# Transposing each head's row maxima one head slot later, and splitting the scaling of v over two slots, in a fused attention and MoE kernel

## The chip, the cores and the metric

The kernel runs on one core of one Trainium2 chip. The metric is the time of one execution in microseconds (us) on the device; the median of a few runs is compared.

The engines are named as in the profile: PE is TensorE's matrix multiplication and PEld its weight loads, DVE is VectorE, ACT is ScalarE, POOL is GpSimd, SP is SyncE, which here only issues transfers. Each engine works through its own list of instructions in order, and waits where an instruction needs a result that another engine or a transfer has not delivered.

## The reference

```python
def _attn_ref(q, k, v):                     # 8 batches, 8 heads, 576 positions, 64 columns
    scores = scale * np.matmul(q, k.transpose(0, 1, 3, 2))
    mask = block_i >= block_j               # blocks of 64 positions
    scores = np.where(mask, scores, -1000000000.0)
    scores = scores - np.max(scores, axis=-1, keepdims=True)
    attn = np.exp(scores)
    attn = attn / (np.sum(attn, axis=-1, keepdims=True) + 1e-09)
    return np.matmul(attn, v).astype(np.float32)

def _moe_ref(x, w_in, w_out):               # 4608 tokens, 512 columns, 2048 inner columns
    h = x @ w_in
    sp = np.maximum(h, 0.0) + np.log1p(np.exp(-np.abs(h)))
    g = h * erf(sp)
    return (g @ w_out).astype(np.float32)
```

The second function gets the first one's result with the heads side by side. Inputs and results are f32; the weights come in as f64.

## The kernel before

Matrix products are made from a high and a low part of each operand, so that three products stand for one. The program has one list of 64 heads (8 batches of 8). For head `n`, `load_qk(n)` brings q and k into one of four buffers `qk0` to `qk3` (`n % 4`), `maxes(n)` makes scores in PSUM (PE, tiles `s01`, `s2`, `s3`, `s4`) and reduces each row to its maximum (DVE, L327, tile `mx`, two of them, used in turn). The last step of `maxes` is `e()`: DVE combines two columns of `mx` (L352), PE transposes `mx` (L354, tile `mt`), ACT copies the result out of PSUM (L356), and ACT issues a transfer of 2.5 KB (L357) that writes it as one more row into the q part of the head's buffer. `probs(n)` then makes the scores again, transposed (PE, L370 and L371, tiles `t0` to `t4`): L370 reads that row, so that the maximum is already subtracted, and ACT takes the exponential (L375). ACT and DVE split the result into a high and a low part (`ph`, L381, and `pl`, L382). `pv` multiplies by v (PE, L414, tile `u`) and sums the rows (PE, L437, tile `us`) for two heads at a time; `normalise` divides, and stores x for the MoE.

v is used in groups of four heads, a quad. `load_v` brings v for a quad into the one buffer `v32`. `prep_v` finds the largest magnitude: a reduction on DVE (L276, tile `vm`), a transpose on PE (L278, `vt`), three small DVE instructions (L280 to L282, `vs`), then a PE product that broadcasts the value to all partitions (L284, `vb`), a copy by DVE (L286, `vsb`), and the scaled high and low parts `vh` (ACT, L291) and `vl` (DVE, L292). `vl` is the last reader of `v32`, so the next quad's load waits for it.

The main loop goes over head slots `n`. Slot `n` holds the load of head `n + 3`, `maxes(n + 2)`, `probs(n)`, parts of `pv` and `normalise` of earlier heads, the preparation of the first six weight blocks (`w1`, slots 1 to 8), and a step of `moe1`. In `merge`, each list of steps is spread over a stretch of the slot (from `lo` to `hi`, 0 to 1 unless said). A scheduler then decides each engine's order of instructions: it takes an instruction early where it believes its inputs ready, so MoE matmuls (L154, tile `m_h`, and L164, tile `o`) of later steps stand between those of attention. After the heads comes the rest of the first MoE pass, with six of the sixteen weight blocks, and then the second pass with the other ten. While no x is there, `warm` matmuls (L510) that compute nothing fill PE.

Of the kernel before, what the change touches and what calls it, by code (L numbers as in the profile page):

```python
# [34 lines left out]
def tile_attention_moe(ctx: ExitStack, tc: tile.TileContext, qk, v, w, maskrows, sels, out):  # L35
# [10 lines left out]
    NQ = H // 4  # L46
# [131 lines left out]
    def merge(*lists):  # L178
        for step in merged(*lists):
            step()  # L180
# [11 lines left out]
    N = B * H  # L192
# [46 lines left out]
    with tc.tile_pool(name="apool", bufs=2) as apool, tc.tile_pool(name="spool", bufs=1) as spool, \  # L239
# [17 lines left out]
        def bank(name):  # L257

            turn.append(0)
            k = len(turn) % 8 if not xs1 else 0  # L260
            if k in (2, 5):
                return ps_h.tile([P, 512], F32, tag="h", name=name)
            if k in (3,):
                return ps_o.tile([P, 512], F32, tag="o", name=name)
            return ps_a.tile([P, 512], F32, tag="a", name=name)

        def load_v(b, qd):
            v32 = apool.tile([P, 4, 5 * D], F32, tag="v32", name=f"v32_{b}_{qd}", bufs=1)
            nc.sync.dma_start(v32, v[b, :, 4 * qd : 4 * qd + 4, :])
            return v32  # L270

        def prep_v(b, qd, v32):

            nm = f"{b}_{qd}"
            vm = apool.tile([P, 1], F32, tag="vm", name=f"vm{nm}")
            nc.vector.tensor_reduce(out=vm, in_=v32, axis=AX.XY, op=ALU.max, apply_absolute_value=True)  # L276
            pt = bank(f"vt{nm}")
            nc.tensor.transpose(out=pt[:1, :P], in_=vm, identity=ident)  # L278
            vs = apool.tile([1, 2], F32, tag="vs", name=f"vs{nm}")
            nc.vector.tensor_reduce(out=vs[:, :1], in_=pt[:1, :P], axis=AX.X, op=ALU.max)  # L280
            nc.vector.tensor_scalar(out=vs[:, :1], in0=vs[:, :1], scalar1=1e-30, op0=ALU.max, scalar2=None)
            nc.vector.reciprocal(out=vs[:, 1:2], in_=vs[:, :1])  # L282
            pb = bank(f"vb{nm}")
            nc.tensor.matmul(pb[:, :2], lhsT=onesrow, rhs=vs, start=True, stop=True)  # L284
            vsb = apool.tile([P, 2], F32, tag="vsb", name=f"vsb{nm}", bufs=3)
            nc.vector.tensor_copy(vsb, pb[:, :2])  # L286
            vh = apool.tile([P, 4, 5, D], F16, tag="vh", name=f"vh{nm}")
            vl = apool.tile([P, 4, 5, D], F16, tag="vl", name=f"vl{nm}")
            vf = v32.rearrange("p a b -> p (a b)")
            vhf = vh.rearrange("p a b c -> p (a b c)")  # L290
            nc.scalar.activation(vhf, vf, AF.Copy, scale=vsb[:, 1:2])  # L291
            nc.vector.scalar_tensor_tensor(out=vl.rearrange("p a b c -> p (a b c)"), in0=vf, scalar=vsb[:, 1:2], in1=vhf,  # L292
                                           op0=ALU.mult, op1=ALU.subtract)
            return vsb, vh, vl
# [5 lines left out]
        def load_qk(n):  # L300
            b, h = divmod(n, H)
            t = qks[n % NB][:, : 4 * S].rearrange("p (i n) -> p i n", n=S)
            st = apool.tile([P, S], F32, tag="st", name=f"st_{n}", bufs=3)

            def a():
                nc.sync.dma_start(st, qk[b, h])
                nc.gpsimd.dma_start(t[:D, 2:4, :], qk[b, h].rearrange("(s d) n -> d s n", d=D))
                nc.sync.dma_start(f32(t[D:, 0:2, :]), f32(t[:D, 2:4, :]))
                nc.sync.dma_start(f32(t[:D, 1, :]), f32(t[:D, 3, :]))

            def c():
                nc.gpsimd.tensor_tensor(out=t[:D, 0, :], in0=st[:D, :], in1=f32(t[:D, 2, :]), op=ALU.subtract)  # L312
                nc.gpsimd.tensor_tensor(out=t[D:, 1, :], in0=st[D:, :], in1=f32(t[D:, 1, :]), op=ALU.subtract)  # L313

            return a, c
# [160 lines left out]
        vs, prs, usbs = {}, {}, {}  # L476
        normals, ready_at, ready = {}, {}, 0
        for n in range(NB - 1):
            for f in load_qk(n):
                f()  # L480
        v32 = load_v(0, 0)
        vs[0] = prep_v(0, 0, v32)
        for f in maxes(0) + maxes(1):
            f()
        def late(kind, steps):

            def run(f):
                tc.cur_priority += PRIO.get(kind, 0)
                f()
                tc.cur_priority -= PRIO.get(kind, 0)  # L490
            return [lambda f=f: run(f) for f in steps]
# [23 lines left out]
        for n in range(N + 4):  # L515
            lists = []
            if n + NB - 1 < N:
                load, low = load_qk(n + NB - 1)
                lists += [(late("load", [load]), 0, LQ), (late("low", [low]), LQ, 1)]
            if n + 2 < N:  # L520
                lists.append((late("max", maxes(n + 2)), 0, 1))
            if n < N:
                prs[n] = []
                lists.append((late("prob", probs(n, prs[n])), 0, 1))
            qd = n // 4 + 1
            if n % 4 == 1 and qd < N // 4:
                v32 = load_v(*divmod(qd, NQ))
            if n % 4 == 2 and qd < N // 4:
                lists.append((late("v", [lambda qd=qd: vs.__setitem__(qd, prep_v(*divmod(qd, NQ), v32))]), 0, 1))
            if n % 2 == 0 and 2 <= n <= N:  # L530
                j = n // 2 - 1
                qd, pp = divmod(j, 2)
                usbs[j] = apool.tile([P, S], F32, tag="usb", name=f"usb{j}", bufs=3)
                steps = pv(qd, pp, [prs.pop(2 * j), prs.pop(2 * j + 1)], vs[qd], usbs[j], rss[j % 3])
                lists.append((late("pv", steps[0]), 0, 1))
                later = late("pv", steps[1])
                if pp == 1:
                    normals[n + 1] = qd
            elif n % 2 == 1 and 2 < n <= N + 1:
                lists.append((later, 0, 0.6 if n in normals else 1))  # L540
            if n in normals:
                qd = normals.pop(n)
                b, q_ = divmod(qd, NQ)
                lists.append((late("norm", normalise(b, q_, [usbs.pop(2 * qd), usbs.pop(2 * qd + 1)], [rss[2 * qd % 3], rss[(2 * qd + 1) % 3]])), 0.6, 1))
                if q_ == NQ - 1:
                    ready_at[n + 1] = (b + 1) * S // T
            ready = ready_at.get(n, ready)
            for _ in range(W1.count(n)):
                lists.append((late("w1", [next_w1]), 0, 1))
            for _ in range(W2.count(n - N)):  # L550
                lists.append((late("w2", [early_w2]), 0, 1))
            k = RATE if n < N else RATE2
            if not xs1:
                lists.append(([warm] * WARM, 0, 1))
            lists.append((late("moe", [lambda: moe1(ready, LAG)] * k), 0, 1))
            merge(*lists)
# [92 lines left out]
```

## Time and profile before

| what | value |
|---|---|
| median of 3 runs | 1390.43 us (1387.09 to 1399.27) |
| the profiled execution | 1395.17 us |
| its span, first to last instruction | 1393.3 us |
| busy share of PE, DVE, ACT, POOL | 91 %, 57 %, 70 %, 42 % |
| mean granted TensorE clock | 0.951 of full speed |

The time of a run holds a little more than the span of its instructions (1395.17 against 1393.3). Busy shares are over the whole span; the stretch in which heads are processed reaches to about 700 us, and the MoE passes follow. The granted clock is a share of 2.4 GHz; 0.50 of it is the lower of its two levels, 1.2 GHz.

### The profile page before, as it was taken

What the parts mean: (1) busy time and instruction counts of PE and PEld (TensorE: products, weight loads), DVE (VectorE), ACT (ScalarE), POOL (GpSimd) and SP (SyncE); (2) the same over time, 40 slices, a digit from 0 to 9 for tenths busy, and PEclk for the clock granted to TensorE, in tenths of its full rate; (3) what the DMA queues carried; (4) which work ended last, traced back from release to release, by engine and by line L of the source; (5) the groups of instructions that cost most, each with busy time, mean ns of one, the idle gap of its engine ahead of it and who ended that gap; (6) DMA issues with size and microseconds to landing.
All of it is one profiled execution on the core that took longest, in us unless ns stands there. A gap on an engine that the chain in (4) does not pass through costs nothing. (4 is left out here: it accounts for less than half of the span.)

```text
span 1393.3 us, 22087 instructions
## 1 busy us (share of the span) xinstructions
PE 1271.2 (91%) x8198; PEld 1027.8 (74%) x8198; DVE 793.9 (57%) x1237; ACT 979.8 (70%) x1781; POOL 587.8 (42%) x456
## 2 busy tenths in 40 slices
PE   3788799899999987999898998689999999999998
PEld 1555578677778776777677887578888888888887
DVE  5769877677677777777865226963233232332332
ACT  1546578677778766778667776587777777777775
POOL 3857655445445544445455224652222222222221
PEclk9989799898899999999799999999999999999999
DMA  9457656756666657567245423303113212311110
GB/s 238 124 153 199 182 146 170 205 155 174 188 165 190 172 147 182 161 185 181 82 138 204 164 91 106 121 0 121 61 61 106 77 61 73 109 61 61 61 61 31
DMA packets 89371, 179.96 MB, mean 129 GB/s; under 512 B 8540, under 2 KB 27292, under 8 KB 89264
## 3 DMA queue, kind: packets, MB, share of 16 engines
q1 hardware_dynamic: 79280, 159.41, 38.3%
q0 software_dynamic: 9344, 18.97, 6.1%
q8 instruction: 65, 1.06, 0.3%
q10 hardware_dynamic: 640, 0.17, 0.1%
q14 instruction: 42, 0.34, 0.1%
HBM read 112.29 MB, written 37.75 MB: 108 GB/s over the span
## 5 line engine op out<-in xcount | busy, mean ns | idle before, releaser
L128 ACT ACTIVATE m_r<-m_r,c 128x512 f32<-128x512 f32 x576 | 414.7, 722 | 112.4 <-DVE m_r L130 97.1
L137 POOL TENSOR_TENSOR m_gl<-m_r,m_gh 128x512 fp32r<-128x512 f32 x144 | 195.3, 1357 | 457.3 <-ACT m_gh L136 426.1
L130 DVE SCALAR_TENSOR_TENSOR m_r<-m_r,m_r 128x512 f32<-128x512 f32 x144 | 118.9, 826 | 323.9 <-ACT m_r L128 318.4
L154 PE MATMUL m_h<-xh,whi 128*128 128x256 f32 (+1 forms) x648 | 214.9, 332 | 8.4 <-DVE m_r L135 8.4
L154 PE MATMUL m_h<-xl,whi 128*128 128x256 f32 (+1 forms) x648 | 213.0, 329 | 1.4 <-DMA xl<-x_d 1.4
L327 DVE TENSOR_REDUCE mx<-s 64x1 f32<-64x288 f32 (+4 forms) x384 | 169.6, 470 | 75.2 <-PE s L324 71.8
L154 PE MATMUL m_h<-xh,wlo 128*128 128x256 f32 (+1 forms) x648 | 211.9, 327 | 0.0
L375 ACT ACTIVATE p<-t 128x288 f32<-128x288 f32 (+4 forms) x384 | 143.2, 388 | 78.0 <-PE t L371 62.9
L164 PE MATMUL o<-whi,m_gh 128*128 128x512 f32 x432 | 172.5, 399 | 9.4 <-ACT m_gh L136 4.8
L164 PE MATMUL o<-wlo,m_gh 128*128 128x512 f32 x432 | 171.8, 398 | 0.0
L382 DVE TENSOR_TENSOR pl<-p,ph 128x832 f16<-128x832 f32 (+1 forms) x128 | 152.2, 1190 | 28.6 <-ACT ph L381 28.2
L312 POOL TENSOR_TENSOR qk<-st,qk 64x576 fp32r<-64x576 f32 x64 | 97.7, 1526 | 144.6 <-PE s L324 41.8
L154 PEld LDWEIGHTS m_h<-xh,whi 128*128 128x128 f32 x648 | 128.0, 197 | 30.1 <-DVE m_r L135 11.4
L164 PE MATMUL o<-whi,m_gl 128*128 128x512 f32 x432 | 147.7, 394 | 1.3 <-POOL m_gl L137 1.3
L370 PE MATMUL t<-qk 69*128 69x288 f32 (+4 forms) x384 | 136.5, 356 | 6.3 <-ACT mt L356 2.6
L135 DVE SCALAR_TENSOR_TENSOR m_r<-m_r,m_h 128x512 f32<-128x512 f32 x144 | 98.3, 683 | 75.2 <-ACT m_r L128 75.0
L154 PEld LDWEIGHTS m_h<-xl,whi 128*128 128x128 f32 x648 | 127.7, 197 | 16.7 <-DMA xl<-x_d 1.7
L324 PE MATMUL s<-qk 68*128 68x256 f32 (+3 forms) x384 | 127.8, 365 | 13.1 <-DMA qk<-qk 7.9
L313 POOL TENSOR_TENSOR qk<-st,qk 64x576 fp32r<-64x576 f32 x64 | 105.3, 1645 | 73.8 <-DMA qk<-qk 72.0
L154 PEld LDWEIGHTS m_h<-xh,wlo 128*128 128x128 f32 x648 | 127.6, 197 | 9.5 <-issue 0.3
L371 PE MATMUL t<-qk 128*128 128x288 f32 (+4 forms) x384 | 131.2, 342 | 0.0
L136 ACT CAST m_gh<-m_r 128x512 fp32r<-128x512 f32 x144 | 89.0, 618 | 50.3 <-DVE m_r L135 49.5
(83 smaller groups left out, 2378.3 us busy)
## 6 DMA issues: line engine op xcount, KB each, us to landing
st<-qk SPq DMA_DIRECT2D x64, 288.0 KB
qk<-qk POOLq DMA_DIRECT2D x64, 288.0 KB, 4.4
qk<-qk SPq DMA_DIRECT2D x64, 288.0 KB
x_d<-xs SPq DMA_DIRECT2D x32, 576.0 KB
raw<-w SPq DMA_DIRECT2D x32, 512.0 KB
v<-v SPq DMA_DIRECT2D x16, 640.0 KB
qk<-qk SPq DMA_DIRECT2D x64, 144.0 KB
xh<-x_d SPq DMA_DIRECT2D x18, 512.0 KB
```

Of the source, the lines that this page charges most:

```text
L128: nc.scalar.activation(r, regs[o[1]], AF.Square, bias=const(pp[1]), scale=pp[0])
L130: nc.vector.scalar_tensor_tensor(out=r, in0=regs[o[1]], scalar=pp[0], in1=regs[o[2]], op0=ALU.add, op1=ALU.mult)
L137: nc.gpsimd.tensor_tensor(out=gl, in0=g, in1=f32(gh), op=ALU.subtract)
L154: nc.tensor.matmul(h[:, k, :], lhsT=a[:, 0, sl], rhs=x[:, cc, :], start=cc == 0 and i == 0, stop=cc == NCC - 1 and i == 2)
L164: nc.tensor.matmul(o[c], lhsT=a[:, sl], rhs=b_[:, 1, :], start=first and k == 0 and not lo and b_ is whi, stop=last and k == nu - 1 and lo)
L313: nc.gpsimd.tensor_tensor(out=t[D:, 1, :], in0=st[D:, :], in1=f32(t[D:, 1, :]), op=ALU.subtract)
L324: nc.tensor.matmul(dst[:r, :w_], lhsT=qh[:K, i * P : i * P + r], rhs=kh[:K, k0 : k0 + w_], start=True, stop=True)
L327: nc.vector.tensor_reduce(out=mx[:r, col : col + 1], in_=src, axis=AX.X, op=ALU.max, negate=True)
L370: nc.tensor.matmul(s[:kk, :w_], lhsT=kh[:K, ks], rhs=qh[:K, q0 : q0 + w_], start=True, stop=False)
L371: nc.tensor.matmul(s[:kk, :w_], lhsT=klh[:, ks], rhs=qhl[:, q0 : q0 + w_], start=False, stop=True)
L375: nc.scalar.activation(p32s[part][:kk, c : c + w_ - skip], s[:kk, skip:w_], AF.Exp, scale=SCALE)
L382: nc.vector.tensor_tensor(out=pl, in0=p, in1=ph, op=ALU.subtract)
```

## The change

The last step `e()` of `maxes` is taken off its list and kept in `rows`. `maxes(n + 2)` in slot `n` now ends with the last reduction; the combination, the transpose, the copy and the transfer of head `n + 2` are put into the first 0.6 of slot `n + 1`, the slot before the one that uses the row. Before the loop, the maxima of heads 0 and 1 are made first and only head 0's row is finished; head 1's is left to slot 0. `prep_v` is split: `scale_v` (reduction, transpose, the three small instructions) stays in slots with `n % 4 == 2`, and the rest (broadcast, `vsb`, `vh`, `vl`) goes to the following slot, `n % 4 == 3`. No instruction is added or removed. In the changed kernel line numbers behind L270 are larger: L327 is L335, L352 is L360, L354 is L362, L356 is L364, L370 is L378, L382 is L390, L284 is L292, L292 is L300.

```diff
-        def prep_v(b, qd, v32):
+        vs_ = {}
+
+        def scale_v(b, qd, v32):
             nm = f"{b}_{qd}"
             vm = apool.tile([P, 1], F32, tag="vm", name=f"vm{nm}")
...
             vs = apool.tile([1, 2], F32, tag="vs", name=f"vs{nm}")
+            vs_[qd + NQ * b] = vs
             nc.vector.tensor_reduce(out=vs[:, :1], in_=pt[:1, :P], axis=AX.X, op=ALU.max)
             nc.vector.tensor_scalar(out=vs[:, :1], in0=vs[:, :1], scalar1=1e-30, op0=ALU.max, scalar2=None)
             nc.vector.reciprocal(out=vs[:, 1:2], in_=vs[:, :1])
+
+        def prep_v(b, qd, v32):
+
+            nm = f"{b}_{qd}"
+            vs = vs_.pop(qd + NQ * b)
             pb = bank(f"vb{nm}")
...
         v32 = load_v(0, 0)
+        scale_v(0, 0, v32)
         vs[0] = prep_v(0, 0, v32)
-        for f in maxes(0) + maxes(1):
-            f()
+        rows = {}
+        for n in range(2):
+            *steps, rows[n] = maxes(n)
+            for f in steps:
+                f()
+        rows.pop(0)()
...
             if n + 2 < N:
-                lists.append((late("max", maxes(n + 2)), 0, 1))
+                *steps, rows[n + 2] = maxes(n + 2)
+                lists.append((late("max", steps), 0, 1))
+            if n + 1 in rows:
+                lists.append((late("max", [rows.pop(n + 1)]), 0, 0.6))
...
             if n % 4 == 2 and qd < N // 4:
+                lists.append((late("v", [lambda qd=qd: scale_v(*divmod(qd, NQ), v32)]), 0, 1))
+            if n % 4 == 3 and qd < N // 4:
                 lists.append((late("v", [lambda qd=qd: vs.__setitem__(qd, prep_v(*divmod(qd, NQ), v32))]), 0, 1))
```

Since a scheduler sets the order, the change shows in the order of the built programs. On PE, around the transpose of head 33 (`mt33`), in the kernel before; `s4_33_1` is the last score product of that head, `t1_31` and `t2_31` are products of head 31's probabilities, `o1` are MoE products:

```order
L371 MATMUL t4_31_320_4244<-qk3_101 64x256
L324 MATMUL s4_33_1_4252<-qk1_99 64x288
L164 MATMUL o1_3_0_8521<-wlo0_326,m1_3_0_gh_8559 128x512
L370 MATMUL t1_31_128_4255<-qk3_101 128x448
L371 MATMUL t1_31_128_4255<-qk3_101 128x448
L164 MATMUL o1_3_0_8521<-whi1_456,m1_3_0_gh_8559 128x512
L164 MATMUL o1_3_0_8521<-wlo1_457,m1_3_0_gh_8559 128x512
L164 MATMUL o1_3_0_8521<-whi0_325,m1_3_0_gl_8560 128x512
L164 MATMUL o1_3_0_8521<-whi1_456,m1_3_0_gl_8560 128x512
L354 MATMUL mt33_4279<-ident_77,mx1_127 5x128
L370 MATMUL t2_31_256_4284<-qk3_101 128x320
L371 MATMUL t2_31_256_4284<-qk3_101 128x320
```

Seven matmuls stand between the last scores of the head and the transpose of its maxima. On PE, around the same transpose in the changed kernel, where it has moved behind a score product of head 34 (`s2_34`) into the next slot:

```order
L422 LDWEIGHTS vh3_1_3726
L422 MATMUL u7_1_0_4301<-pl1_30_4175,vh3_1_3726 64x128
L332 MATMUL s2_34_4312<-qk2_100 128x384
L362 MATMUL mt33_4316<-ident_77,mx1_127 5x128
L378 MATMUL t3_32_320_4321<-qk0_98 128x256
L379 MATMUL t3_32_320_4321<-qk0_98 128x256
L154 MATMUL m1_4_0_h_8685<-xh256_1024_8486,whi1_448 128x256
L154 MATMUL m1_4_0_h_8685<-xl256_1024_8488,whi1_448 128x256
```

There are now 37 matmuls between the head's last scores and the transpose; before there were seven. On PE in the changed kernel, the stretch ahead of `t0_32`, the first product that reads the row of head 32, whose transpose `mt32` stands 27 matmuls earlier:

```order
L332 MATMUL s4_33_1_4275<-qk1_99 64x288
L164 MATMUL o1_3_0_8521<-wlo0_326,m1_3_0_gh_8559 128x512
L378 MATMUL t2_31_256_4278<-qk3_101 128x320
L379 MATMUL t2_31_256_4278<-qk3_101 128x320
L154 MATMUL m1_4_0_h_8685<-xh256_1024_8486,whi0_325 128x256
L154 MATMUL m1_4_0_h_8685<-xl256_1024_8488,whi0_325 128x256
L154 MATMUL m1_4_0_h_8685<-xh256_1024_8486,wlo0_326 128x256
L154 MATMUL m1_4_0_h_8685<-xh256_1024_8486,whi0_325 128x256
L154 MATMUL m1_4_0_h_8685<-xl256_1024_8488,whi0_325 128x256
L154 MATMUL m1_4_0_h_8685<-xh256_1024_8486,wlo0_326 128x256
L378 MATMUL t0_32_0_4292<-qk0_98 128x288
L379 MATMUL t0_32_0_4292<-qk0_98 128x288
```

In the kernel before 69 matmuls stood between `mt32` and `t0_32`; now there are 27. On DVE, around the combination of head 33's maxima in the kernel before; `vm4_1` is the reduction of the next quad's v, `pl0_31` the low part of head 31's probabilities:

```order
L327 TENSOR_REDUCE mx1_127<-s4_33_0_4241 64x1
L327 TENSOR_REDUCE mx1_127<-s4_33_1_4252 64x1
L276 TENSOR_REDUCE vm4_1_4581<-v32_4_1_4407 128x1
L382 TENSOR_TENSOR pl0_31_4249<-p32_0_117,ph0_31_4248 128x832
L352 TENSOR_TENSOR mx1_127<-mx1_127 64x1
L135 SCALAR_TENSOR_TENSOR m1_3_1_r1_8612<-m1_3_1_r1_8612,m1_3_1_h_8573 128x512
```

On DVE in the changed kernel, at the same place:

```order
L335 TENSOR_REDUCE mx1_127<-s4_33_0_4249 64x1
L335 TENSOR_REDUCE mx1_127<-s4_33_1_4275 64x1
L360 TENSOR_TENSOR mx1_127<-mx1_127 64x1
L300 SCALAR_TENSOR_TENSOR vl4_0_4224<-v32_4_0_3916,vsb4_0_4221,vh4_0_4223 128x1280
L390 TENSOR_TENSOR pl0_31_4246<-p32_0_117,ph0_31_4245 128x832
L335 TENSOR_REDUCE mx0_126<-s01_34_4296 128x1 x2
```

The combination now follows the last reduction directly. The reduction `vm4_1` has moved behind it, to the slot of head 34's maxima, and `vl4_0` stands where the combination was waited for.

## Rows read from the trace of the kernel before

**Rows 1.** The page: busy time, share of the span and instructions of each engine.

```profile
PE 1271.2 (91%) x8198; PEld 1027.8 (74%) x8198; DVE 793.9 (57%) x1237; ACT 979.8 (70%) x1781; POOL 587.8 (42%) x456
```

**Rows 2.** Busy time by stretch: length, five engines' busy us, granted clock, DMA share, GB/s.

```profile
0.00:50.00 50.00, 22.02 (x79) 13.27 (x80) 31.03 (x55) 13.93 (x27) 26.98 (x43) 0.93 0.73 192
50.00:200.00 150.00, 127.20 (x993) 88.80 (x991) 122.71 (x204) 91.03 (x198) 99.88 (x67) 0.87 0.61 166
200.00:700.00 500.00, 457.67 (x3910) 374.98 (x3914) 369.69 (x619) 372.15 (x787) 249.05 (x192) 0.94 0.63 168
900.00:1393.00 493.00, 484.36 (x2120) 399.72 (x2118) 162.74 (x232) 358.04 (x537) 128.29 (x98) 0.99 0.20 67
```

**Rows 3.** PE's waits, 50 to 720 us: total us, times, longest.

```profile
PE mt L354 <- DVE mx L352: 35.7, 24, 5.7
PE u L414 <- DVE pl L382: 8.8, 5, 5.2
PE vb L284 <- DVE vs L282: 4.0, 4, 2.4
```

**Rows 4.** Timeline of DVE, then PE, around head 33's transpose: start, us, instruction, [idle before].

```profile
366.62 0.45 DVE L327 TENSOR_REDUCE mx<-s 64x1 f32<-64x288 f32 x1 [0.40 <-PE s L324]
367.61 1.49 DVE L276 TENSOR_REDUCE vm<-v 128x1 f32<-128x1280 f32 x1 [0.54 <-DMA v<-v]
369.01 1.01 DVE L382 TENSOR_TENSOR pl<-p,ph 128x832 f16<-128x832 f32 x1
369.94 0.14 DVE L352 TENSOR_TENSOR mx<-mx 64x1 f32<-64x1 f32 x1
...
367.54 0.62 PE L164 MATMUL o<-whi,m_gl 128*128 128x512 f32 x2
370.23 0.27 PE L354 MATMUL mt<-ident,mx 128*5 128x128 f32 x1 [2.07 <-DVE mx L352]
```

**Rows 5.** Busy time by stretch, as rows 2: before and after that transpose, and behind another.

```profile
361.90:371.90 10.00, 7.93 (x70) 6.20 (x69) 8.36 (x14) 8.64 (x20) 2.70 (x2) 1.00 0.78 202
371.90:382.10 10.20, 10.20 (x67) 8.18 (x68) 4.70 (x8) 5.98 (x15) 4.00 (x5) 0.50 0.76 195
...
290.40:300.60 10.20, 9.37 (x105) 6.71 (x105) 7.91 (x14) 8.10 (x18) 3.44 (x4) 1.00 0.65 170
```

**Rows 6.** Sum of the eight stretches at half clock beside a transpose's wait, 330 to 697 us.

```profile
sum 54.50, PE 51.36 PEld 41.10 DVE 36.87 ACT 28.35 POOL 23.38; mean PE 6.42 PEld 5.14 DVE 4.61 ACT 3.54 POOL 2.92
```

**Rows 7.** Timeline, head 0's transpose, copy, transfer, and the first matmul that reads the row.

```profile
31.78 0.42 PE L354 MATMUL mt<-ident,mx 128*5 128x128 f32 x1
...
32.23 0.26 ACT L356 CAST mt<-mt 5x128 fp32r<-5x128 f32 x1 [7.00 <-PE mt L354]
32.52 1.28 ACTq L357 DMA_DIRECT2D qk<-mt  x1
...
36.28 0.37 PE L370 MATMUL t<-qk 69*128 69x288 f32 x1 [0.19 <-DMA qk<-mt]
```

**Rows 8.** Transfers by tile: count, KB each, median us from issue to landing where known.

```profile
qk<-qk POOLq DMA_DIRECT2D x64, 288.0 KB, 4.4
...
qk<-mt ACTq DMA_DIRECT2D x64, 2.5 KB
```

**Rows 9.** Timeline of PE at full clock: 256-column MoE matmuls, and one set of row sums.

```profile
306.07 0.28 PE L154 MATMUL m_h<-xh,whi 128*128 128x256 f32 x1
306.19 0.29 PE L154 MATMUL m_h<-xl,whi 128*128 128x256 f32 x1
306.32 0.28 PE L154 MATMUL m_h<-xh,wlo 128*128 128x256 f32 x1
306.43 0.28 PE L154 MATMUL m_h<-xh,whi 128*128 128x256 f32 x1
...
58.46 0.34 PE L437 MATMUL us<-ph,ones 128*32 128x384 f16 x4
...
59.39 0.41 PE L370 MATMUL t<-qk 69*128 69x320 f32 x1
```

**Rows 10.** Timeline of SP, v's load for that quad; SP's wait for it, 50 to 720 us.

```profile
361.67 0.33 SPq L269 DMA_DIRECT2D v<-v  x1
...
SPq L269 <- DVE vl L292: 21.4, 11, 3.8
```

**Rows 11.** Timeline of POOL at the start, around the load of head 4.

```profile
41.93 1.26 POOL L108 TENSOR_TENSOR wlo<-sq,bits 128x512 fp32r<-128x512 f32 x1
...
45.36 0.62 POOL L307 DMA_DIRECT2D qk<-qk  x1
46.05 1.52 POOL L312 TENSOR_TENSOR qk<-st,qk 64x576 fp32r<-64x576 f32 x1
```


## The prediction

> **What bounds the kernel now.** I read the page's busy shares first: PE is busy 91 % of the span, the next engine 70 % [rows 1]. Then the busy time by stretch, because that share is a mean over stages: from 200 to 700 us, where the heads run at an even pace, PE is busy 457.7 of 500 us and the others at most 372.2, and the granted clock is 0.94 of full speed; before 200 us no engine is near full; from 900 us on PE is busy 484.4 of 493 at clock 0.99 [rows 2]. So among the heads PE is the bound, but it loses time in two ways that its share hides: 42 us of idle in those 500, and 0.06 x 500 = 30 us to the half clock. PE's work is the same in both kernels, and idle time taken from it while the heads run is taken from the total, since the MoE work that the scheduler now leaves for later runs on a PE that is never idle for long.
>
> The view of who waits for whom says what the idle is: 35.7 us in 24 waits ahead of the transpose of the row maxima, released by DVE's combination of them; 4.0 us ahead of the broadcast of v's magnitude; 8.8 us ahead of `u`, which the change doesn't touch [rows 3]. One place in the timeline shows why. Head 33's last maximum is reduced at 366.6 to 367.1, then DVE waits 0.54 us for v's load, reduces v (1.49 us), makes a low part (1.01) and only then combines the maxima (0.14, at 369.94). PE ran out of work at 368.2, and its transpose stands at 370.23, idle 2.07 us before [rows 4]. What is queued behind the transpose on PE doesn't need it.
>
> **The clock.** In the 10 us up to that transpose the granted clock is 1.00, in the 10.2 us behind it 0.50, that is 1.2 GHz in place of 2.4; behind the transpose at 290.36, whose wait was shorter (1.66), it stays 1.00 [rows 5]. I find eight such stretches beside a transpose that waited 1.5 us or longer, 54.5 us in all at a mean clock of 0.50 [rows 6]; at half clock half of it is lost, some 27 us. So the wait costs more than its own length, as far as the longer ones go.
>
> **The change, part by part.**
>
> *The transpose is moved behind other work.* By the order, head 33's transpose has 37 matmuls between the head's last scores and itself where it had seven. At 0.12 us for 256 columns and 0.93 us for a set of row sums [rows 9], seven matmuls (3,456 columns) are 1.6 us of work and the 37 some 4.4; over the heads from 9 on the mean goes from 2.0 to 4.0 us. DVE was late by 1.6 + 2.07 = 3.7 us at head 33, and the 2.5 us of `vm` and `pl` that stood ahead of the combination [rows 4] now stand behind it. So I take the 35.7 us as gone. The reduction of v is now ahead of the combination of the next head's maxima (`mx0`, head 34), which has 3.7 us of work as cover: priced at nothing. If v came some 2 us later than now, that cover would be gone, and the same 2 us would be back at one transpose in four.
>
> *The broadcast one slot later.* The small DVE chain that it waits for is then long done: 4.0 us gone. `vh` and `vl` come a slot later, and `vl` frees `v32`: SP's queue waited 21.4 us in 11 times for `vl` ahead of v's load [rows 10], with the copies of q and k and the loads of `st` behind it. In SP's order v's load has itself moved behind two copies and two loads of x, so I take nothing for it; PE doesn't need this `v` for two slots.
>
> *What is late next: the row.* Four steps follow the transpose: ACT's copy, ACT's issue, the transfer, and the first matmul that reads the row. This chain was covered before: by the order 5 to 13 us of matmul work stood between transpose and reader. Now it is 3.9, 3.8 and 3.9 us (means over the heads with n % 4 of 0, 1 and 3) and 7.0 us for the fourth. Head 32 is an example: 27 matmuls with 8,258 columns, 3.9 us. With the clock of this stretch, 0.94, and so 7 % more, 4.1 us. What the chain takes is seen once, at head 0: transpose at 31.78, copy at 32.23 (0.26), issue at 32.52, and the reader at 36.28, released by that transfer [rows 7]: 4.5 us, of which 0.74 until the issue and 3.8 for issue and landing. The transfer could be quicker where the DMA engines are less loaded (share 0.73 in the first 50 us, 0.63 later [rows 2]), or as slow as the big loads, 4.4 us [rows 8], and ACT's copy can stand behind another ACT instruction. The excess over the cover lies between 0 (landing within 3.3 us of the issue) and 1.0 us (0.74 + 4.4 - 4.1); head 0's value gives 0.4, and since a short chain gives nothing back and a long one costs, I take 0.6. There are 41 heads with the short cover from head 9 on: 41 x 0.6 = 25 us (0 to 41).
>
> The Trainium skill, in "DMA: Bandwidth & Descriptors", section "Anatomy of one DMA", puts the fixed part of a transfer at about 2.0 us, nearly all of it the confirmation of the write. By that price an estimate of the chain is 0.74 + 2.0 = 2.7 us, all covered, and the 25 us would be 0. The same page's section "Issuing engines are not separate DMA queues" says that ACT's transfers run on the same engines as all others and interleave with them, which speaks against a flat 2.0 here; head 0's row agrees with the second.
>
> *The clock's part.* The new waits are many and short, 0.4 to 1.0 us, where the clock fell beside waits of 1.5 us or longer. But a scatter about a 4.5 us chain will bring some of that length. Of the 27 us I take 10 as given back (0 to 27).
>
> *The start.* DVE now has 7 more weight-preparing instructions ahead of head 2's maxima, and on POOL head 4's load, issued at 45.36, now stands behind two more weight steps and two subtractions for head 3, about 1.3 and 1.5 us each [rows 11]: 5.5 us later. The weights come earlier in exchange, and PE is idle or filled with `warm` for much of this stretch (127 of 150 us busy from 50 to 200, at clock 0.87 [rows 2]). I take 0, between 5 us less and 5 us more.
>
> **The sum.** Against the profiled execution of 1395.2 us (span 1393.3): 1395.2 - 35.7 - 4.0 + 25 - 10 = 1370.5. That execution was 4.7 us above the median of the runs (1390.4), so for a median I take 1366.
>
> **Rivals.**
>
> *The row is covered* (0.17). If it lands within 3.3 us of its issue, no new wait appears, and the clock has no cause to fall: 1395.2 - 39.7 - 27 - 4.7 = 1324. For it: a row is 2.5 KB [rows 8], and the engines' share is 0.63, not 1. Against it: the only row that shows the chain. The skill's fixed price, above, would give this case.
>
> *The wait is traded one for one* (0.18). The row takes as long as the big loads: 41 us of new waits, and no clock given back: 1395.2 - 39.7 + 41 - 4.7 = 1392.
>
> *The maxima are still late* (0.08). DVE, busy 370 of 500 us [rows 2], stays behind by the length of the new cover because v's load now lands later; about half of the old wait remains beside the row's: 1395.2 - 22 + 25 - 5 - 4.7 = 1389. Against it: nothing but the reductions is left ahead of three combinations in four.
>
> *Slower: the row queues behind v's load* (0.12). v's load was issued at 361.67 [rows 10] and DVE could start on it at 367.61 [rows 4]: 5.9 us. It is now issued at the end of a slot, shortly before head 33's row and its like. If one row in each quad takes 0.74 + 5.9 us, it is 2.5 us late (14 quads: 35 us), and with the other 27 short heads at 1.0 that is 62 us; waits of 2.5 us bring the half clock each time, 14 times some 3.4 us against the 27 of now: 21 us more. 1395.2 - 39.7 + 62 + 21 - 4.7 = 1434. It decides as soon as the new waits pass 39.7 us, that is 0.97 us for each of the 41 heads; my 0.6 isn't far from that.
>
> **How the numbers follow.** The forecast has 0.45, with 1352 to 1381 as its own range (new waits of 0.4 to 0.9 us). From the median 1390.4, 1 % either way, about what a measurement of this kernel can tell from no change, is 1376.5 and 1404.3. Faster by more: 0.38 of the forecast and the covered row, 0.55. Within 1 %: the rest of the forecast, nearly all of the even trade and of the late maxima, 0.30. Slower: 0.15, the last rival and the upper ends of the two before it. The range, 1334 to 1400, leaves out most of the slower rival and half of the covered row.
>
> **What the next profile would show.** Waits of PE at the transpose near 0 in place of 35.7, and at the broadcast in place of 4.0. A new row of waits at L378 (`t`), released by the transfer of `mt` or by ACT, of some 25 us. The granted clock from 200 to 700 us at 0.95 to 0.97 in place of 0.94, PE busy some 470 in a stretch of 500. DVE's wait for v's load unchanged in length but with nobody waiting behind it. What would make the prediction wrong: row waits above 40 us, a clock that falls as often as before, or a start in which the first twelve heads take more than 5 us longer.

## The result, and the profile after

| | before | after |
|---|---|---|
| median of 20 runs each, us | 1401.12 (1387.09 to 1415.45) | 1379.31 (1365.60 to 1396.00) |
| ratio of after to before, 95 % interval | | 0.9865 [0.9835, 0.9896] |
| profiled execution, us | 1395.17 | 1378.77 |
| its span, us | 1393.3 | 1377.0 |
| mean granted clock | 0.951 | 0.96 |

The changed kernel is 1.35 % faster. Executions more than 1.5 % above the fastest one of the same kernel count as slow and are left out of every ratio, so 0.9865 is not the quotient of the two medians. The kernel before has a median of 1401 us over 20 runs where the first three gave 1390; so the forecast is best read as a ratio: 1366 / 1390.4 = 0.982 against 0.9865.

The page's busy shares after the change answer to [rows 1]; PE's share goes from 91 to 93 %:

```profile
PE 1277.7 (93%) x8198; PEld 1021.0 (74%) x8198; DVE 782.0 (57%) x1237; ACT 971.7 (71%) x1781; POOL 599.3 (44%) x456
```

The busy time by stretch of the changed kernel, as [rows 2], shows where the time came from:

```profile
0.00:50.00 50.00, 16.99 (x62) 9.32 (x63) 31.86 (x50) 10.94 (x19) 26.42 (x43) 0.94 0.71 186
50.00:200.00 150.00, 137.57 (x1045) 94.87 (x1044) 126.67 (x212) 94.57 (x210) 100.78 (x70) 0.88 0.64 175
200.00:700.00 500.00, 472.25 (x4011) 374.08 (x4009) 369.63 (x635) 375.61 (x809) 272.34 (x197) 0.96 0.64 171
```

Between 200 and 700 us PE is busy 14.6 us longer than in [rows 2], at clock 0.96 in place of 0.94, and issues 4011 matmuls in place of 3910. Nothing was added to the program: it is the same work done earlier. PE's visible idle from 50 to 700 us falls from 650 - 127.2 - 457.7 = 65.1 to 650 - 137.6 - 472.3 = 40.1 us, that is by 25 us, although the waits that the change was to remove came to 39.7. The view of who waits for whom, 50 to 720 us, as [rows 3], tells what came in their place:

```profile
PE t L378 <- DMA qk<-mt: 8.2, 8, 2.2
PE t L378 <- DVE mx L335: 6.7, 5, 2.9
PE s L332 <- DVE mx L335: 6.6, 6, 4.4
...
PE rb L475 <- ACT rw L470: 4.1, 5, 1.7
PE mt L362 <- ACT usb L425: 3.3, 3, 2.3
PE u L422 <- DVE pl L390: 3.0, 3, 1.1
...
PE mt L362 <- DVE mx L360: 1.8, 5, 0.5
```

The transpose waits 1.8 us for the combination where it waited 35.7; the broadcast has no row. New are 8.2 us at the reader of the row, released by its transfer, and 6.7 us at the same line released by DVE. The groups by line from 200 to 700 us (count, busy us, mean ns, idle before and its releasers) say the same of line L370 in the kernel before,

```profile
L370 PE MATMUL t<-qk 69*128 69x288 f32 (+4 forms) x288 | 98.7, 343 | 0.7 <-ACT p L375 0.2
```

and of L378, the same line of the changed kernel:

```profile
L378 PE MATMUL t<-qk 69*128 69x288 f32 (+4 forms) x291 | 99.3, 342 | 14.2 <-DMA qk<-mt 7.8 <-DVE mx L335 4.9 <-DVE vl L300 0.7
```

One row that came late is that of head 21. The timeline of the changed kernel around it:

```profile
243.52 1.08 SPq L269 DMA_DIRECT2D v<-v  x1
...
244.50 0.27 PE L362 MATMUL mt<-ident,mx 128*5 128x128 f32 x1
...
244.70 0.47 SPq L316 DMA_DIRECT2D qk<-qk  x1
...
245.41 0.72 ACTq L365 DMA_DIRECT2D qk<-mt  x1
...
251.84 0.55 PE L378 MATMUL t<-qk 69*128 69x288 f32 x1 [2.23 <-DMA qk<-mt]
```

v's load (640 KB) was issued 1.9 us ahead of the row and q and k of a later head 0.7 us ahead; the row was there 6.4 us after its issue, where head 0's took 3.8 [rows 7], and the whole chain from the transpose took 7.3. Of the eight waits of this kind, the four longest (2.23, 1.53, 1.01 and 1.55 us, so 6.3 of the 8.2) are at heads with n % 4 = 1 (21, 41, 57, 61). At the first three v's load was issued within 2 us of the row. At head 61 it was not: the last load of v stands 47 us ahead of that row, which yet was there only 4.9 us after its issue; two loads of x (512 KB each, the first shown) were issued 0.5 and 0.1 us ahead of it:

```profile
601.84 0.41 SPq L269 DMA_DIRECT2D v<-v  x1
...
648.76 0.38 SPq L187 DMA_DIRECT2D xh<-x_d  x1
...
649.24 0.70 ACTq L365 DMA_DIRECT2D qk<-mt  x1
...
654.11 0.37 PE L378 MATMUL t<-qk 69*128 69x288 f32 x1 [1.55 <-DMA qk<-mt]
```

So a late row does not need v's load near it, and no run moves a load alone.

Of the waits at L378 that DVE released, the longest has another cause. Around it, the timeline of the changed kernel shows DVE, and PE's first matmul behind the wait:

```profile
609.04 1.49 DVE L278 TENSOR_REDUCE vm<-v 128x1 f32<-128x1280 f32 x1 [5.57 <-DMA v<-v]
610.45 1.74 DVE L390 TENSOR_TENSOR pl<-p,ph 128x832 f16<-128x832 f32 x1
612.11 0.44 DVE L335 TENSOR_REDUCE mx<-s 64x1 f32<-64x288 f32 x1
...
612.60 0.40 PE L378 MATMUL t<-qk 69*128 69x288 f32 x1 [2.93 <-DVE mx L335]
```

DVE stands still for 5.57 us because the reduction of v is next in its list and v isn't there; `pl` and the last reduction of the head's scores, whose inputs are ready, queue behind it, and PE's next product is released only by that reduction. (Behind the others, 1.30 us and less from 200 us on, DVE is busy throughout and merely late.) The same happened at a larger price three quads earlier, ahead of a score product: it is the longest of the waits at L332 above, 6.6 us in all.

```profile
483.74 1.49 DVE L278 TENSOR_REDUCE vm<-v 128x1 f32<-128x1280 f32 x1 [5.47 <-DMA v<-v]
...
487.60 0.80 PE L332 MATMUL s<-qk 68*128 68x256 f32 x2 [4.38 <-DVE mx L335]
```

The two together cost PE 7.3 us. DVE's waits for v's load, 50 to 720 us, before and after:

```profile
DVE vm L276 <- DMA v<-v: 14.1, 7, 4.2
...
DVE vm L278 <- DMA v<-v: 18.8, 6, 5.6
```

The clock by stretch, some ten us ahead of and behind the waits at 251.8 and 612.6 us, as [rows 5], and behind the one at 487.6:

```profile
251.80:262.00 10.20, 10.14 (x73) 7.94 (x74) 6.83 (x13) 5.57 (x13) 5.70 (x4) 0.83 0.76 193
241.80:251.80 10.00, 7.37 (x70) 4.88 (x70) 5.22 (x7) 5.42 (x13) 3.27 (x3) 1.00 0.85 205
612.60:622.60 10.00, 7.74 (x33) 7.08 (x34) 5.38 (x10) 5.31 (x12) 3.52 (x3) 0.55 0.35 98
602.00:612.60 10.60, 6.67 (x83) 4.79 (x81) 4.60 (x6) 3.73 (x11) 4.65 (x4) 1.00 0.69 167
...
487.60:497.60 10.00, 9.30 (x33) 7.89 (x34) 4.01 (x9) 5.69 (x13) 4.25 (x3) 0.50 0.46 125
```

### The profile page after: what moved, and what is told of

Read it like the earlier page. It is cut to its first block, busy times and chain, and to the rows that moved or that the text cites. A ratio compares the mean times of both kernels' runs of the same rounds, so it can differ in the third digit from the quotient of the medians.

```text
span 1377.0 us, 22100 instructions
## 1 busy us (share of the span) xinstructions
PE 1277.7 (93%) x8198; PEld 1021.0 (74%) x8198; DVE 782.0 (57%) x1237; ACT 971.7 (71%) x1781; POOL 599.3 (44%) x456
## 5 line engine op out<-in xcount | busy, mean ns | idle before, releaser
L130 DVE SCALAR_TENSOR_TENSOR m_r<-m_r,m_r 128x512 f32<-128x512 f32 x144 | 111.7, 776 | 331.2 <-ACT m_r L128 326.2
L335 DVE TENSOR_REDUCE mx<-s 64x1 f32<-64x288 f32 (+4 forms) x384 | 170.2, 468 | 67.2 <-PE s L332 64.7
L164 PE MATMUL o<-wlo,m_gh 128*128 128x512 f32 x432 | 174.7, 404 | 0.0
L390 DVE TENSOR_TENSOR pl<-p,ph 128x832 f16<-128x832 f32 (+1 forms) x128 | 161.4, 1262 | 21.3 <-ACT ph L389 20.7
L332 PE MATMUL s<-qk 68*64 68x288 f32 (+3 forms) x384 | 132.2, 364 | 25.0 <-DVE mx L335 17.1
L164 PE MATMUL o<-whi,m_gl 128*128 128x512 f32 x432 | 152.4, 403 | 1.5 <-POOL m_gl L137 1.5
L378 PE MATMUL t<-qk 69*128 69x288 f32 (+4 forms) x384 | 134.7, 352 | 18.5 <-DMA qk<-mt 9.9
L154 PEld LDWEIGHTS m_h<-xh,whi 128*128 128x128 f32 x648 | 125.4, 193 | 34.3 <-DVE m_r L135 19.5
L320 POOL TENSOR_TENSOR qk<-st,qk 64x576 fp32r<-64x576 f32 x64 | 99.2, 1550 | 105.2 <-PE t L379 27.2
L321 POOL TENSOR_TENSOR qk<-st,qk 64x576 fp32r<-64x576 f32 x64 | 113.6, 1776 | 70.6 <-DMA qk<-qk 68.0
L379 PE MATMUL t<-qk 128*128 128x288 f32 (+4 forms) x384 | 123.9, 324 | 0.0
```

The costliest lines, as they stand in the source:

```text
L130: nc.vector.scalar_tensor_tensor(out=r, in0=regs[o[1]], scalar=pp[0], in1=regs[o[2]], op0=ALU.add, op1=ALU.mult)
L154: nc.tensor.matmul(h[:, k, :], lhsT=a[:, 0, sl], rhs=x[:, cc, :], start=cc == 0 and i == 0, stop=cc == NCC - 1 and i == 2)
L164: nc.tensor.matmul(o[c], lhsT=a[:, sl], rhs=b_[:, 1, :], start=first and k == 0 and not lo and b_ is whi, stop=last and k == nu - 1 and lo)
L332: nc.tensor.matmul(dst[:r, :w_], lhsT=qh[:K, i * P : i * P + r], rhs=kh[:K, k0 : k0 + w_], start=True, stop=True)
L335: nc.vector.tensor_reduce(out=mx[:r, col : col + 1], in_=src, axis=AX.X, op=ALU.max, negate=True)
L378: nc.tensor.matmul(s[:kk, :w_], lhsT=kh[:K, ks], rhs=qh[:K, q0 : q0 + w_], start=True, stop=False)
```

## The experiments

Every ratio is to the kernel before, run beside the experiment on the same chip, with a 95 % interval. The theory: the transposes carry the gain, since PE no longer waits for DVE, and what it gives back lies at the row. The rivals: the split of v carries it; or the size of the gain is set at the start, not in the even stretch, that is among the evenly paced heads. A ratio comes from several executions; a trace shows one of them.

**One half of the change each.** The transposes alone (`rows_only`), v's preparation whole in slots with n % 4 = 2 as before:

```diff
-                lists.append((late("v", [lambda qd=qd: scale_v(*divmod(qd, NQ), v32)]), 0, 1))
-            if n % 4 == 3 and qd < N // 4:
-                lists.append((late("v", [lambda qd=qd: vs.__setitem__(qd, prep_v(*divmod(qd, NQ), v32))]), 0, 1))
+                lists.append((late("v", [lambda qd=qd: (scale_v(*divmod(qd, NQ), v32), vs.__setitem__(qd, prep_v(*divmod(qd, NQ), v32)))]), 0, 1))
```

> The transposes one slot later, v's scaling in one slot as before. Theory (the gain comes from the transposes that no longer wait, which takes 33 us of PE's waits at L362 away and with them half-clock time, while short waits at the next matmuls take most of it back): waits at the transpose under 8 us, half clock from 200 to 700 us under 50 us, ratio to the kernel before 0.985 to 0.992. Rival (the split of v's scaling does it, since it takes the reduction of v from ahead of the combination of maxima): ratio 0.997 to 1.003, and 20 us or more of waits left at the transpose or at the scores.

The split of v alone (`v_only`), the transposes as before:

```diff
...
-                *steps, rows[n + 2] = maxes(n + 2)
-                lists.append((late("max", steps), 0, 1))
-            if n + 1 in rows:
-                lists.append((late("max", [rows.pop(n + 1)]), 0, 0.6))
+                lists.append((late("max", maxes(n + 2)), 0, 1))
```

> v's broadcast one slot later, the transposes as before. Theory: only the 4.0 us of waits at the broadcast go, the transposes still wait 25 us or more, ratio 0.995 to 1.003. Rival (the split of v's scaling does it): waits at the transpose under 15 us, ratio 0.985 to 0.992.

Measured: `rows_only` 0.993 [0.9899, 0.9961], `v_only` 0.9959 [0.9931, 0.9988]; their product, 0.989, lies inside the interval of the whole change. In `v_only` the transposes wait as before, 50 to 720 us:

```profile
PE mt L362 <- DVE mx L360: 34.3, 28, 5.6
```

`rows_only` has lost these waits, yet gained only half of what the whole change did. Its busy time by stretch says where the rest is:

```profile
50.00:200.00 150.00, 130.89 (x892) 87.41 (x893) 116.50 (x188) 81.74 (x179) 89.97 (x62) 0.79 0.57 155
200.00:700.00 500.00, 475.30 (x4049) 385.39 (x4048) 371.31 (x640) 381.75 (x816) 268.43 (x200) 0.96 0.66 173
```

In the even stretch it is as good as the whole change; from 50 to 200 us its clock is 0.79 (0.87 before) and it issues 892 matmuls (993 before). So the start had to be separated from the rest.

**Start and even stretch apart.** With the change in the prologue and slots 0 to 11 only (`start_only`), and from slot 12 on only (`late_only`, shown without its last lines, which put the split of v under `n >= 12`):

```diff
-        for n in range(2):
-            *steps, rows[n] = maxes(n)
...
+        for f in maxes(0) + maxes(1):
+            f()
...
-                *steps, rows[n + 2] = maxes(n + 2)
+                steps = maxes(n + 2)
+                if n >= 12:
+                    rows[n + 2] = steps.pop()
...
+            if n % 4 == 2 and qd < N // 4 and not (n >= 12):
+                lists.append((late("v", [lambda qd=qd: (scale_v(*divmod(qd, NQ), v32), vs.__setitem__(qd, prep_v(*divmod(qd, NQ), v32)))]), 0, 1))
...
```

> The change in the prologue and slots 0 to 11 alone; as before from slot 12 on. Theory (gain in the even stretch): ratio 0.995 to 1.008, waits at the transpose of 25 us or more. Rival (gain from the start): ratio 0.985 to 0.992.

> The change from slot 12 on alone; slots 0 to 11 and the prologue as before. Theory (the gain is made while the heads run at an even pace; the first 200 us only add or take some half clock by chance of the order): ratio 0.985 to 0.992, waits at the transpose from 200 to 700 us under 10 us. Rival (the gain comes from the start): ratio 0.996 to 1.003.

Measured: `start_only` 1.0051 [1.0016, 1.0085], `late_only` 0.9815 [0.977, 0.986]. Their product is 0.9865, the ratio of the whole change: all of the gain comes from slot 12 on, more of it than I expected, and the start costs half a per cent. `late_only` by stretch, and its waits:

```profile
200.00:700.00 500.00, 477.23 (x4063) 380.42 (x4063) 379.82 (x645) 384.12 (x822) 279.51 (x203) 0.97 0.64 177
```

```profile
PE vb L292 <- DVE vs L285: 3.6, 2, 2.7
PE t L378 <- DMA qk<-mt: 3.3, 5, 1.0
PE mt L362 <- DVE mx L360: 2.3, 4, 1.5
```

The broadcast's wait is back, 3.6 of the 4.0 us: it belongs to the first slots, in which `late_only` is written as the kernel before. What the start costs is not seen in the start of `start_only`:

```profile
0.00:50.00 50.00, 16.39 (x61) 8.78 (x61) 32.64 (x49) 10.94 (x19) 25.60 (x42) 0.93 0.73 186
50.00:200.00 150.00, 139.46 (x1062) 96.76 (x1062) 129.76 (x215) 97.73 (x213) 101.99 (x70) 0.88 0.62 170
200.00:700.00 500.00, 449.05 (x3790) 369.27 (x3790) 361.05 (x604) 363.32 (x765) 245.23 (x188) 0.92 0.61 166
```

By 200 us it has issued 1123 matmuls where the kernel before has 1072. It falls behind afterwards, where its steps are written as in the kernel before: 44.2 us of waits at the transposes in place of 35.7, and clock 0.92 in place of 0.94, one execution of each. Why those heads wait longer behind a faster start wasn't found.

**The halves again, from slot 12 on.** `late_rows_only` is `late_only` with v's preparation whole throughout; `late_v_only` is `late_only` with the transposes as before throughout. The edits are those of the first pair, on `late_only`.

> Only the transposes of the maxima are moved, and only from slot 12 on; v's preparation is whole in one slot as in the kernel before, and the start is the one of the kernel before. Theory: the move of the transposes carries the gain of the even stretch and the split of v is an accompaniment: ratio to the kernel before 0.979 to 0.988, PE's waits ahead of the transpose for DVE's combination under 8 us (35.7 before), the granted clock from 200 to 700 us at 0.96 or 0.97. Rival: the split of v is needed too, since otherwise the broadcast of v and the combination behind the reduction of v keep PE waiting: ratio 0.990 or more, and the waits at the broadcast of 4 us or more remain.

> Only v's preparation is split over two slots, and only from slot 12 on; the transposes stay where the kernel before has them. Theory: the split takes the broadcast's 4 us away and nothing else: ratio 0.993 to 1.000, waits ahead of the transpose still 25 us or more in 50 to 720 us. Rival: the split alone gives a good part of the gain, since the reduction of v no longer keeps the combination back: ratio 0.988 or less, waits ahead of the transpose under 20 us.

Measured: `late_rows_only` 0.986 [0.9812, 0.9909], `late_v_only` 1.0023 [0.9986, 1.0059]. The transposes carry the gain, although 4.2 us of waits at the broadcast remain in `late_rows_only`; the split of v alone gives nothing here. Whether it adds something to the transposes (0.9815 against 0.986) the intervals don't decide. The waits of `late_rows_only`,

```profile
PE t L378 <- DVE mx L335: 8.1, 3, 7.5
...
PE mt L362 <- DVE mx L360: 4.7, 5, 2.0
PE t L378 <- DMA qk<-mt: 4.3, 5, 1.6
```

and of `late_v_only`:

```profile
PE mt L362 <- DVE mx L360: 34.9, 18, 6.1
```

The 7.5 us in the first of these are v's load again, as at 484 and 609 us above; DVE and PE in the timeline of `late_rows_only`:

```profile
488.06 1.49 DVE L278 TENSOR_REDUCE vm<-v 128x1 f32<-128x1280 f32 x1 [7.64 <-DMA v<-v]
...
490.19 0.64 PE L378 MATMUL t<-qk 69*128 69x320 f32 x1 [7.48 <-DVE mx L335]
```

**How far the transposes are moved.** The finishing steps are spread over the first 0.6 of the slot. Five kernels change this number alone: `row002`, `row03` and `row10` the whole change with 0.04, 0.3 and 1.0, and `late_row05` and `late_row10` `late_only` with 0.5 and 1.0:

```diff
-                lists.append((late("max", [rows.pop(n + 1)]), 0, 0.6))
+                lists.append((late("max", [rows.pop(n + 1)]), 0, 0.3))
```

> As the changed kernel, with the transposes at the very beginning of the following slot (0 to 0.04): 1.7 to 2.3 us of matmul work ahead of the transpose, as in the kernel before, and 6.8 to 9.9 behind it. Theory (a transpose waits where the work ahead of it is short, and L378 waits where the work behind it is short): waits at the transpose of 20 us or more again, L378's waits on the row under 2 us, ratio 0.995 to 1.005. Rival (L378's new waits come from DVE and PSUM banks, not from the row): L378 still waits 10 us or more in all.

> As the changed kernel, with the transposes spread over the first 0.3 of the following slot in place of 0.6: by the order 1.8 to 3.3 us of matmul work ahead of the transpose (3.6 to 4.7 in the changed kernel) and 4.9 to 7.7 behind it, up to the matmul that reads the row (3.8 to 7.0). Theory (the waits at the row are paid for by short covers): waits of L378 on the row fall from 8.2 to under 3 us, waits at the transpose stay under 10 us, ratio 0.98 to 0.987. Rival (the maxima are late, and the cover ahead of the transpose is what counts): waits at the transpose over 15 us, ratio 0.99 to 1.0.

> As the changed kernel, with the transposes spread over the whole following slot (0 to 1.0): 4.5 to 6.2 us of matmul work ahead of the transpose, 3.3 to 6.5 behind it. Theory: the row becomes the wait, L378 waits 20 us or more on it, ratio 0.99 to 1.0. Rival (cover ahead of the transpose is what counts): L378 waits as in the changed kernel, 8 us, ratio 0.98 to 0.987.

> The change from slot 12 on, with the finishing of the maxima in the first 0.5 of the slot. By the order the transposes of heads 16 to 63 have 3.0 to 3.5 us of matmul work ahead and 3.8, 5.6, 8.0 and 4.9 us behind them until the row is read. Theory: both chains are covered here, so it is at least as fast as the version with 0.6 (0.9815): ratio 0.976 to 0.984, waits ahead of the transpose under 6 us and at the row under 4 us. Rival: the cover ahead is what counts, and with less of it the transposes wait again as they did with 0.3: waits ahead of the transpose of 10 us or more, ratio 0.986 or more.

> The change from slot 12 on, with the finishing of the maxima spread over the whole slot instead of its first 0.6. By the order the transposes of heads 16 to 63 then have 4.6 to 6.1 us of matmul work ahead of them and 3.3 to 3.7 us (7.0 for one in four) between them and the reader of the row, against 3.6 to 4.4 and 3.9 (7.4) with 0.6. Theory: the row's cover sets the time once the transposes are covered: the waits of the reader for the row's transfer are 8 us or more from 50 to 720 us, and the ratio is 0.985 to 1.000, above the one of the version with 0.6. Rival: the loss that the same setting showed over the whole program (1.011) came from the first 200 us, and the even stretch doesn't mind: ratio 0.978 to 0.985.

The cover is the matmul work that the order puts ahead of the transpose (behind the head's last scores) and behind it (until the row is read), at 0.12 us for 256 columns [rows 9]; means over heads 16 to 63 with n % 4 = 0, 1, 2, 3. Waits are from 50 to 720 us.

| kernel | cover ahead, us | cover behind, us | transpose waits for the combination, us | reader waits for the row, us | ratio |
|---|---|---|---|---|---|
| before | 1.6, 2.4, 1.7, 2.3 | 8.6, 6.7, 11.8, 10.0 | 35.7 | none | 1 |
| `row002` | 1.7, 2.0, 2.3, 2.4 | 7.2, 8.2, 9.9, 6.8 | 43.6 | 1.6 | 1.0031 [0.9993, 1.0069] |
| `row03` | 1.9, 3.6, 3.1, 3.2 | 4.8, 5.7, 7.8, 5.6 | 19.7 | 5.3 | 1.0017 [0.9988, 1.0046] |
| after (0.6) | 3.6, 4.4, 3.8, 4.1 | 3.9, 3.9, 7.4, 4.0 | 1.8 | 8.2 | 0.9865 [0.9835, 0.9896] |
| `row10` | 4.7, 6.1, 4.7, 4.6 | 3.7, 3.4, 7.0, 3.4 | 1.1 | 9.7 | 1.0112 [1.0071, 1.0153] |
| `late_row05` | 3.0 to 3.5 | 3.8, 5.6, 8.0, 4.9 | 15.1 | 1.9 | 0.9892 [0.9843, 0.9941] |
| `late_only` (0.6) | nearly as after | nearly as after | 2.3 | 3.3 | 0.9815 [0.977, 0.986] |
| `late_row10` | 4.6 to 6.1 | 3.3 to 3.7, 7.0 | 5.3 | 9.3 | 0.9943 [0.9908, 0.9978] |

The waits at the transpose follow the cover ahead: with some 2 us the transposes wait 35 to 44 us, with about 3 us 15 to 20, with about 4 us or more 1 to 5. The row's waits follow the cover behind only at its ends, none to 1.6 us with the longest and 9.3 to 9.7 with the shortest; between them `row03` waits 5.3 us with more cover than `late_row05`, which waits 1.9, and `late_only` 3.3 with nearly that of the changed kernel, which waits 8.2. Nor do these two waits make the time alone: `row03` has 25 us of them in place of 35.7 and gains nothing (1.0017).

At 0.3 and at 0.5 I expected both chains to be covered and was wrong; the rival, that less cover ahead brings the transposes' wait back, is what the waits show. For `row10` neither expectation held: the row waits 9.7 us, not 20 or more, and yet the ratio is above both ranges. A row came late without v's load here too: in `row03` that of head 20 was there 6.2 us after its issue, with no load of v in the 35 us before it, but with two loads of x issued 1.2 and 0.7 us ahead.

```profile
249.53 0.36 SPq L187 DMA_DIRECT2D xh<-x_d  x1
...
250.68 0.70 ACTq L365 DMA_DIRECT2D qk<-mt  x1
...
256.92 0.37 PE L378 MATMUL t<-qk 69*128 69x288 f32 x1 [1.41 <-DMA qk<-mt]
```

At 1.0 there is a loss in the late version too (0.9943 against 0.9815, some 18 us), of which the row's longer wait shows 6 us (9.3 against 3.3); the rest, up to 1.0112, comes with the start, where `row10` runs from 50 to 200 us at clock 0.77:

```profile
50.00:200.00 150.00, 132.05 (x895) 90.25 (x894) 109.86 (x186) 82.44 (x182) 95.32 (x62) 0.77 0.59 157
```

**DVE's part of the wait.** If the transposes waited because `vm` (1.49 us) stood ahead of the combination [rows 4], a smaller `vm` in the kernel before should shorten them. `vm_small_before` reduces 64 of v's 1280 columns, a twentieth; so v's scale is computed from part of v.

```diff
-            nc.vector.tensor_reduce(out=vm, in_=v32, axis=AX.XY, op=ALU.max, apply_absolute_value=True)
+            nc.vector.tensor_reduce(out=vm, in_=v32[:, :, :16], axis=AX.XY, op=ALU.max, apply_absolute_value=True)
```

> The kernel before, with the magnitude of v taken from 64 of its 1280 columns, so that the reduction of v on DVE is some 0.2 us in place of 1.49 (the output is scaled by a magnitude of part of v). Theory (the transposes waited because v's load and reduction stood ahead of the combination of maxima on DVE): waits at the transpose fall from 35.7 to under 22 us, ratio 0.987 to 0.997. Rival (the transposes wait because only 1.5 to 2.4 us of matmul work stand ahead of them, whatever DVE does in between): waits of 28 us or more, ratio 0.997 to 1.003.

Measured: 0.9921 [0.9886, 0.9956], and the waits at the transposes 25.8 us:

```profile
PE mt L354 <- DVE mx L352: 25.8, 20, 2.8
```

The ratio is what the theory had, and 0.8 % is more than half of what the whole change gives: the reduction of v is part of DVE's lateness. The waits, down by 9.9 us, lie between what theory and rival had. Its profiled execution, 1400.40 us, was the longest of its twelve, so the waits are less firm than the ratio, and how much of the lateness is something else stays open.

## Why the prediction was right, and where it was not

**The bound and the transposes: right.** The move took 35.7 us of waits down to 1.8, and PE issues its work earlier by it. `late_rows_only` shows that this step carries the gain: with it alone the ratio is 0.986. That it does so through the waits fits the kernels that keep them: `v_only` (34.3 us), `late_v_only` (34.9) and `row002` (43.6) have 0.9959, 1.0023 and 1.0031. But fewer waits at the transpose are not enough, as `row03` shows.

**The broadcast: right.** The 4.0 us are gone, and the split alone gives 0.9959 over the whole program, that is 2 to 10 us by its interval. As 3.6 of the 4.0 us lie in the first slots, it gives nothing from slot 12 on (1.0023).

**The row: sized at 25 us, and too large; the sum came near it by another cause.** I had forecast some 25 us of waits at L378 released by the transfer of the row or by ACT; the transfer released 8.2. All idle ahead of L378 grew by 13.5 us from 200 to 700 us. That is only what the profile shows as idle: a stall shorter than the modelled end of the matmul before it (0.28 us where the next one starts 0.12 us later [rows 9]) doesn't show. An estimate with those, the distance between matmul starts less the column time at the granted clock, has the stall ahead of this line grow from some 13 to some 37 us, by 22 to 24 as one counts the smallest. That this is nearly 25 is luck: I had put all of it on the row, and of the visible part the row's transfer released 7.8 of 14.2 us and DVE 4.9.

**DVE behind v's load: priced at nothing, and it costs.** I had written that the reduction of v would stand ahead of the next combination at no price unless v came later, and that nobody would be waiting behind DVE's wait for v. DVE's wait grew from 14.1 to 18.8 us, and two of these waits held PE for 2.93 and 4.38 us; in `late_rows_only` one held it for 7.48.

**The rival that the row queues behind v's load** had 35 us for it. At three heads of the changed kernel (21, 41, 57) a late row does go with v's load, at 1.0 to 2.2 us each, 4.8 us together. Heads 61 here and 20 in `row03` had late rows without it, behind loads of x. Over the traces of the changed kernel and of all versions with moved transposes, nine rows from head 10 on reached a waiting reader more than 5.1 us after their issue, and each had a load of v (640 KB) or x (512 KB) issued within 2 us of it; those without one took 2.9 to 5.0 us. So the rival looked at one kind of big load of two. That such a load makes the row late fits this, but no run moves a load alone, so it isn't shown. From a row's issue to its reader 3.8 us [rows 7] and, at head 21, 6.4 us are measured. The fixed part of about 2.0 us that the Trainium skill states for a transfer issued by GpSimd ("DMA: Bandwidth & Descriptors", section "Anatomy of one DMA") is not what these two, issued by ACT, took, and the covered row, the rival that went with it, did not come.

**The clock: sized at 10 us, measured the same, and not shown to be the transposes' doing.** From 200 to 700 us it goes from 0.94 to 0.96, 0.02 x 500 = 10 us. But over the same stretch `v_only` and `row002`, whose transposes wait as before or longer, have 0.97 and 0.96:

```profile
200.00:700.00 500.00, 455.90 (x3946) 373.36 (x3947) 373.45 (x609) 376.52 (x790) 260.00 (x193) 0.97 0.63 170
...
200.00:700.00 500.00, 455.35 (x3915) 370.33 (x3917) 359.70 (x608) 370.70 (x780) 254.74 (x191) 0.96 0.62 170
```

So the waits at the transposes do not set the clock of the stretch by themselves, as the prediction's sum had it, and that the size came out is luck in part. What is left of the lower clock after the change stands behind other waits: PE still waits 1.5 us or longer six times in this stretch, and over the 10 us behind each of them the clock is 0.50 to 0.83.

**The start: priced at nothing, and it costs.** This is the other term that failed. 1.0051 is 7 us (2 to 12 by its interval), where I had allowed 5 either way; the forecast's ratio was 0.982 against 0.9865 measured, 6 us at 1390, and `late_only`, without the start, has 0.9815. I had looked for them in the first 200 us; in `start_only` they are not lost there, but afterwards, and how is open.

A count that sums all this up is the matmuls issued by 700 us, of the same 8198 in every version: 5182 in `late_only` (span 1364.4 us), 5169 in `late_rows_only` (1373.1), 5118 after (1377.0), 4982 before (1393.3), 4913 in `start_only` (1404.9), 4894 in `row10` (1407.5); the others lie between, not strictly in order. Each is one execution; that of `late_only` (1366.13 us) was the fastest of its six, whose median is 1373.0. What is done under the heads needn't be done behind them. The best version measured is `late_only`, 0.9815; against the changed kernel's 0.9865 its interval just overlaps, and that it is better rests on `start_only` as much as on itself.

## What to carry to other kernels

Where one engine waits for a chain through another engine and a transfer, a step in the middle has cover on both sides, and moving it trades one for the other: work out both covers from the order and compare each with its chain as measured, at its late cases and not at its mean. Look also at what the move puts next in another engine's list: here DVE stood still for a load, and PE waited behind it. Here the best point was narrow: from slot 12 on, 0.6 of the slot gained 1.85 %, 0.5 gained 1.08 (their intervals just overlap) and 1.0 gained 0.57. And try such a change in the even stretch and at the start separately: a version that gains in the even stretch can lose a part of it by how the program gets there.

## What was not expected of the hardware

A transfer of 2.5 KB took 6.4 us from issue to its reader at a DMA share of 0.85, with 640 KB issued 1.9 us ahead of it from another engine's queue; 4.9 and 6.2 us at two heads with two loads of 512 KB issued within 1.2 us ahead of it; and 3.8 us at the start. With the same instructions in another order the granted clock from 50 to 200 us was 0.77 (`row10`), 0.79 (`rows_only`), 0.87 (before) and 0.88 (after), one execution of each. Behind PE's wait of 2.23 us the clock was 0.83 over the next 10.2 us, behind one of 4.38 us 0.50 over the next 10 and behind one of 2.93 us 0.55, with a further wait of 2.26 us in those ten, from 1.00 ahead of all three; before the change, a wait of 1.66 us left it at 1.00 [rows 5]. And 34.3 us of waits at the transposes in `v_only` went with a clock of 0.97, 35.7 us in the kernel before with 0.94.
